# Pooled attention and a gated convolution on one core: the first k load as 32-bit words on SyncE's queue, v of batch 0 pooled on TensorE, and a new order of the queues

## Chip, cores and metric

The kernel runs on one core of one Trainium2 chip. The metric is the device time of one execution in microseconds (us), as the median of several runs. Five engines work side by side, each through its own list of instructions: PE (TensorE, matrix products), DVE (VectorE), ACT (ScalarE), POOL (GpSimd) and SP (SyncE). POOL and SP do almost nothing here but issue transfers (DMAs), which run on 16 DMA engines that all queues share.

## The reference

For each of 8 batches and 8 heads (576 rows, 64 columns), k and v are averaged over groups of 8 rows, so that there are 72 pooled rows. Attention of the 576 rows of q over these gives x; x goes through a gated convolution block.

```
k_p = k.reshape(B, H, Sp, pool, D).mean(axis=3)
v_p = v.reshape(B, H, Sp, pool, D).mean(axis=3)
scores = scale * np.matmul(q, k_p.transpose(0, 1, 3, 2))
attn = softmax(scores)
x = attn @ v_p, heads side by side: 8 x 576 x 512
h = np.maximum(x @ w_in, 0.0)                  # 512 -> 1024
conv_out = three taps along the rows, one weight per column and tap
out = (h * sigmoid(conv_out)) @ w_out          # 1024 -> 512
```

All inputs and the output are 32-bit floats; q, k and v have 9.4 MB each, 1.18 MB per batch.

## The kernel before, in words

**The work of one batch.** POOL issues loads of k, v and q that turn 32-bit floats into bf16 on the way (`load_k` L458, `load_v` L476, `load_q` L433). One row of the tile `k_b` or `v_b` holds a whole group of 8 rows (512 numbers), so pooling is three additions of halves on DVE: 512 to 256 (`pool8`, L632), to 128 (L639), to 64 (L649 for k, L695 for v). There are 576 such rows per batch, so a tile is 128 partitions by 5, with the last column of tiles half filled; rows 64 to 127 of it are zeroed by a memset (L612, L614). PE turns the sums of k (L662), and two copies put them into `kz` (L669), by 64 partitions each. q is regrouped in two halves of four heads (`qg`, L453), turned by PE (L735) and copied to `qT` (L744). Scores are PE products (L767, L769), their exponentials run on ACT (L775), and v enters through `vblk`, the pooled v times a mask (L700, L705). The products of attention and v are L792 and L796 ("av"); DVE divides them (L809, tile xx), PE turns them (L829) and a copy gives `xT` (L835). For late batches SP's transposing DMAs do the turning instead. Then come mm1 (`w_in`, L849 for batch 0 in parts, L872 for the others; relu on ACT), the convolution (on PE by diagonal matrices, L995, or on DVE and ACT, L918 to L945), the gate and its product on DVE into `gT` (L983), and mm2 (`w_out`, L1026) after each pair of batches, copied out of PSUM (L1049, L1039) and stored by SP (L1054, L1044). `gT` has two buffers, one for each second pair of batches; `gT[1]` is first written by batch 2.

**What sets the order.** Every operation is added to a planner (`pl.add`, L136) with a name, an engine, an assumed duration, the keys that it reads and writes, and, for a DMA, the packets. The planner (`order`, L176) picks in assumed time, on each engine, among the operations that can start within 0.02 us of the first one the one with the lowest rank. The ranks are a list of whole numbers, one for each operation in the order of its definition (L17 to L56). Operations that can run on ACT or on DVE (all copies out of PSUM, two of the three taps, the regrouping of q, the diagonal matrices) run on ACT if their names stand in the list "act" (L62), on DVE otherwise. The result is a fixed list of instructions for each engine. Where the assumed time has a gap on PE in the first 60 us, `warm` (L398) puts in products with a tile of zeros (L407), so PE shows no idle time there.

**The start, as it stands in the program.** POOL issues: q's rows 64 to 71, k's large part, k's tail, q's rows 0 to 63, half of v, the identity matrix (`ident`, L525, made by POOL), the tail of v in four, masks, the other half of v, q of batch 1, v's tail of batch 1, the first half of `w_in`, k and v of batch 1, the second half of `w_in`. SP issues the convolution weights (L528) and nothing else before the first store. At most 8 of POOL's loads are assumed to be under way at once (L223).

The lines that the change leans on for v are in the kernel before already, but no batch takes that way (`"vp"` is 0 for all eight):

```
for i in range(TP):
    nc.tensor.matmul(out=a, lhsT=ident, rhs=v_b[m][:, t0:t1, i * D:(i + 1) * D], start=i == 0, stop=i == TP - 1, skip_group_check=True)
...
copy_on(e)(out=vs[:, :, 0:D], in_=slot(key)[:, 0, 0:NT * D].rearrange("p (t d) -> p t d", d=D))
```

Eight products with the identity add up the eight slices of 64 columns in PSUM, in two parts (`vpm.0.0` for two tiles, `vpm.0.1` for three); the copy `vae.0` moves the sum to `vs`.

Of the kernel before, what the change touches and what calls it, by code (L numbers as in the profile page):

```python
# [9 lines left out]
FP32 = mybir.dt.float32  # L10
# [5 lines left out]
PARAMS = {  # L16
    "prio": (  # L17
        "6 14 12 18 16 17 25 33 43 49 53 56 58 61 63 40 38 59 46 54 60 9 32 28 34 31 24 22 "
        "37 29 20 42 39 27 21 35 41 5 2 3 47 11 8 0 30 4 7 13 44 15 36 19 23 10 1 69 "
        "90 75 80 84 62 182 143 45 52 55 57 64 65 51 48 73 78 70 74 26 66 67 77 50 79 72 89 86 "  # L20
        "85 111 88 83 94 82 87 68 71 76 81 93 91 102 126 124 92 115 97 103 112 101 118 99 96 105 98 114 "
        "100 133 119 107 131 109 116 125 113 136 121 110 146 104 141 148 151 157 132 164 120 108 117 106 129 127 123 128 "
        "95 165 174 179 186 189 167 218 172 178 169 173 185 188 175 181 194 201 203 224 234 202 210 211 219 204 184 208 "
        "207 217 221 213 226 233 241 245 231 236 239 244 249 122 130 142 134 150 158 156 161 160 168 152 137 155 138 154 "
        "176 192 135 140 145 149 139 144 147 162 163 170 153 159 171 180 216 200 265 267 220 230 190 196 205 212 193 197 "
        "232 240 247 255 261 266 183 191 177 187 209 225 199 206 195 229 198 237 253 250 277 260 286 293 316 324 328 338 "
        "349 335 355 348 359 370 215 166 223 228 248 257 262 291 304 317 235 214 242 256 238 243 227 222 246 274 287 303 "
        "312 309 321 345 310 327 344 362 334 351 326 340 365 377 381 393 402 380 385 386 411 413 379 387 389 406 412 398 "
        "399 401 408 415 395 400 404 410 417 252 254 289 299 306 320 264 251 270 278 294 322 318 353 292 263 271 305 330 "
        "297 276 302 308 313 339 341 268 273 275 288 300 307 284 283 290 296 311 315 323 258 269 282 285 331 301 280 298 "  # L30
        "329 347 342 350 336 361 371 382 388 384 392 403 407 428 450 461 476 494 507 272 259 295 314 325 319 337 358 369 "
        "374 352 357 360 368 367 376 363 366 281 333 346 343 364 354 418 423 448 457 391 396 427 419 463 451 459 477 480 "
        "484 491 449 489 483 502 528 485 493 495 525 512 501 503 508 522 530 519 524 532 539 542 442 460 488 498 482 506 "
        "475 505 509 520 533 556 576 583 439 444 437 473 447 446 456 478 455 465 469 474 479 486 504 515 429 435 534 541 "
        "443 440 420 454 453 550 552 514 521 529 537 548 569 546 555 570 579 586 591 578 603 616 638 629 685 696 640 656 "
        "674 708 717 279 332 356 375 373 378 383 422 434 426 397 390 414 425 466 470 467 481 464 416 513 452 538 431 421 "
        "430 433 436 511 517 523 531 540 543 497 500 551 549 559 526 564 604 608 590 596 599 610 624 601 607 620 639 647 "
        "611 623 625 642 646 626 631 637 645 641 547 499 568 575 572 585 600 581 584 614 627 630 636 635 573 580 577 561 "
        "588 594 622 598 609 617 652 644 671 675 605 618 562 571 633 612 628 597 643 650 666 651 665 664 593 606 587 595 "
        "634 654 649 632 658 663 673 677 684 676 699 716 721 724 751 746 761 782 756 767 776 784 802 394 409 438 432 424 "  # L40
        "441 445 471 405 487 554 510 592 544 613 496 589 468 615 545 458 462 472 535 565 707 710 718 679 722 729 709 715 "
        "686 694 738 687 736 768 744 692 749 760 743 704 763 798 754 706 759 777 757 732 788 789 667 683 648 659 690 668 "
        "725 680 705 728 731 735 747 809 661 669 681 688 682 697 698 719 720 733 753 765 774 780 657 662 693 703 727 711 "
        "670 714 726 745 739 758 783 795 734 740 712 702 750 742 755 741 769 775 808 810 814 822 845 860 861 872 874 886 "
        "911 903 912 916 518 582 553 574 492 516 527 557 560 567 558 678 566 700 621 372 619 490 563 713 536 653 655 660 "
        "672 785 790 771 779 766 772 773 762 786 801 793 811 804 815 803 812 819 818 806 817 816 825 841 843 846 851 839 "
        "848 850 856 796 807 813 821 824 829 827 823 834 837 835 844 936 855 832 840 826 830 842 828 849 858 847 862 883 "
        "871 885 890 857 863 820 831 865 833 864 836 873 889 888 884 893 898 853 869 838 852 868 854 867 859 876 881 896 "
        "899 905 891 918 926 941 929 948 950 961 972 966 980 969 977 982 602 689 695 770 764 781 748 730 723 752 737 701 "
        "691 778 792 787 878 879 900 917 791 797 800 805 794 799 925 945 931 935 927 930 934 940 937 947 978 959 946 943 "  # L50
        "953 955 956 968 962 967 880 892 895 902 908 913 897 915 919 924 939 928 949 954 906 920 914 951 922 952 944 965 "
        "960 964 971 974 994 983 870 875 882 887 901 904 907 894 923 910 921 932 938 942 866 877 958 963 909 970 957 933 "
        "973 975 984 979 986 989 1010 1019 1014 1021 1025 1023 1032 1038 1041 1055 1005 1012 1000 1004 1008 1009 1015 1007 1020 1018 1024 1022 "
        "1028 1033 981 991 976 985 1027 1034 988 990 993 995 999 1037 1039 1002 1016 992 1001 1030 1035 1003 1011 1006 1013 1017 1045 1042 "
        "996 998 987 997 1046 1044 1026 1029 1031 1036 1040 1047 1048 1043 1051 1052 1059 1050 1053 1049 1056 1054 1058 1060 1071 1057 1061 1062 "
        "1064 1063 1066 1069 1067 1068 1065 1070 "  # L56
# [5 lines left out]
    "act": (  # L62
        "dw1.0 dw1.1 dw4.0 dw5.0 dw6.0 dw6.1 kz.0.0 qg.0.0 qTe.0.0 qTe.0.3 xte.0.2 kz.1.0 "
        "kz.1.1 qg.1.0 qTe.1.0 xte.1.0 xte.1.2 xte.1.4 cp0.0.0 oe.0.0 oe.0.1 oe.0.2 oe.0.3 kz.2.0 "
        "qTe.2.0 qTe.2.1 qTe.2.2 xte.2.0 xte.2.1 xte.2.2 cp2.1.0 cp2.1.4 oe.0.4 oe.0.5 oe.0.6 oe.0.7 "
        "oe.0.8 kz.3.0 qTe.3.0 xte.3.0 xte.3.1 xte.3.2 cp0.2.0 cp0.2.1 cp0.2.3 cp2.2.5 oe.1.0 oe.1.1 "
        "oe.1.2 oe.1.3 kz.4.1 qTe.4.2 xte.4.0 xte.4.1 xte.4.3 cp0.3.0 cp2.3.0 cp2.3.2 cp0.3.4 cp0.3.5 "
        "cp2.3.6 oe.1.5 oe.1.6 oe.1.7 oe.1.8 kz.5.0 kz.5.1 cp2.4.1 cp2.4.3 cp0.4.7 oe.2.2 cp0.5.2 "
# [32 lines left out]
    "qs": [1, 0, 0, 0, 0, 0, 0, 0],  # L101
    "xw": 0,
    "qd": [0, 0, 0, 0, 0, 0, 0, 0],
    "vp": [0, 0, 0, 0, 0, 0, 0, 0],
}


# [7 lines left out]
class Planner:  # L115
# [60 lines left out]
    def order(self):  # L176
# [16 lines left out]
        ring = [0.0] * 4  # L193
# [964 lines left out]
```

## Time and profile before

| | us |
|---|---|
| median of 3 runs | 201.94 |
| lowest and highest of them | 201.72, 202.74 |
| the profiled execution, device time | 200.92 |
| its span, first to last instruction | 199.1 |
| PE busy in it | 190.8 |
| DVE busy in it | 171.0 |
| ACT busy in it | 167.0 |
| granted TensorE clock, share of full speed | 1.00 |

The profile comes from one execution. A row of its timeline gives the start and length of a stretch of like instructions, the engine, the line of the kernel, the operation, the tile written and the tile read, and in brackets how long the engine had been idle before and what released it. "L632" is line 632. The windows give, for each engine, the time that it was busy in a stretch with the number of its instructions, then the granted clock, the share of the 16 DMA engines' time in use (over 1 where packets overlap) and GB/s moved. The chain of work that ended last is followed back from the last instruction to whatever released each one. PE's busy time contains the products with zeros. Loads that convert count their bytes as bf16, half of what they read.

### The profile page before, as it was taken

Reading aid. Unit: us, or ns where it says so; the run is one execution under the profiler, and the core shown is the slowest. Engines: PE = TensorE matmul, PEld = TensorE weight load, DVE = VectorE, ACT = ScalarE, POOL = GpSimd, SP = SyncE. Lnnn points to the kernel's source line nnn. Section 1 sums busy time; section 2 is a strip of 40 time slices with the busy share of each in tenths; the row PEclk is TensorE's granted clock in tenths of the full one; section 3 lists DMA queues with packets and bytes.
Section 4 is the critical chain, followed back from the end, with each engine's and each line's share of the span. In section 5 each row is a group of like instructions: output and inputs, shape, how many; then the busy total and the mean of one; then the engine's idle time right before and its main releaser. Section 6 shows DMA issues by size and latency. Waiting matters only on the chain.

```text
span 199.1 us, 4491 instructions
## 1 busy us (share of the span) xinstructions
PE 190.8 (96%) x1737; PEld 128.9 (65%) x1737; DVE 171.0 (86%) x400; ACT 167.0 (84%) x282; POOL 47.5 (24%) x76
## 2 busy tenths in 40 slices
PE   5999999999999999999999999989999999999992
PEld 5888777777546576767756656547666565765541
DVE  3777999999999999999999999988889997755631
ACT  0677699999995499999999999995999999998410
POOL 7966431543233262761140000000000000000000
PEclk9999999999999999999999999999999999999999
DMA  3999999999999999999999966477112144502324
GB/s 39 185 185 200 204 204 193 207 206 200 195 204 250 268 217 207 159 217 121 113 116 117 70 211 161 85 189 188 28 35 83 65 129 87 211 3 77 135 106 158
DMA packets 52857, 30.00 MB, mean 151 GB/s; under 512 B 33484, under 2 KB 48356, under 8 KB 52836
## 3 DMA queue, kind: packets, MB, share of 16 engines
q0 software_dynamic: 32912, 16.73, 68.1%
q1 hardware_dynamic: 19924, 12.99, 26.9%
q8 instruction: 13, 0.21, 0.4%
q14 instruction: 8, 0.07, 0.1%
HBM read 33.44 MB, written 9.44 MB: 215 GB/s over the span
## 4 chain that ended last, share of the span: by engine, by line
PE 88%; DVE 7%; POOL 2%; DMA 1%; issue 1%; ACT 0%; POOLq 0%
PE psfB L1026 31%; PE psfA L872 25%; PE psfA L792 4%; PE psfA L767 4%; PE psfA L995 4%; PE pswA L407 3%; PE psbB L735 2%; PE psfB L849 2%; DVE xx L809 2%; PE psfA L849 2%; PE psfA L796 2%; PE psbB L829 1%; PE pswB L407 1%; PE psbA L829 1%; DMA xT<-xx 1%; PE psfA L769 1%
## 5 line engine op out<-in xcount | busy, mean ns | idle before, releaser
L1026 PE MATMUL psfB<-w_out,gT 128*128 128x512 bf16 (+1 forms) x282 | 65.5, 378 | 0.0
L872 PE MATMUL psfA<-xT,w_in 128*128 128x288 bf16 x448 | 59.2, 286 | 0.9 <-DMA xT<-xx 0.7
L872 PEld LDWEIGHTS <-w_in 128*128 128x128 bf16 x448 | 42.8, 98 | 14.8 <-issue 1.2
L1026 PEld LDWEIGHTS <-gT 128*128 128x128 bf16 x290 | 27.2, 98 | 29.0 <-issue 0.2
L878 ACT ACTIVATE hT<-psfA 128x576 bf16<-128x576 f32 x56 | 35.2, 651 | 2.2 <-PE psfA L872 2.0
L918 ACT ACTIVATE cv<-hT,cr 128x576 bf16<-128x576 bf16 x37 | 28.3, 779 | 0.2
L809 DVE TENSOR_TENSOR xx<-psfA,rr 128x512 bf16<-128x512 f32 (+1 forms) x40 | 26.8, 683 | 0.9 <-DMA xT<-xx 0.7
L920 DVE TENSOR_SCALAR cv<-hT,cr 128x576 bf16<-128x576 bf16 x71 | 23.9, 363 | 3.9 <-ACT tg L945 2.3
L775 ACT ACTIVATE attnT<-psfA 128x576 bf16<-128x576 f32 x40 | 25.1, 674 | 0.3 <-PE psfA L767 0.2
L983 DVE TENSOR_TENSOR gT<-tg,hT 128x1152 bf16<-128x1152 bf16 x32 | 23.7, 750 | 1.2 <-ACT tg L1002 0.8
L927 DVE TENSOR_TENSOR cv<-cv,hT 128x1152 bf16<-128x1152 bf16 (+1 forms) x31 | 20.8, 672 | 4.0 <-ACT cv L918 3.9
L945 ACT ACTIVATE tg<-cv,cn 128x576 bf16<-128x576 bf16 x31 | 23.2, 775 | 0.9 <-DVE cv L937 0.6
L937 DVE TENSOR_TENSOR cv<-cv 128x1152 bf16<-128x1152 bf16 (+1 forms) x31 | 20.8, 673 | 0.2
L1049 ACT COPY osb<-psfB 128x512 f32<-128x512 f32 x24 | 14.3, 595 | 7.4 <-PE psfB L1026 7.3
L945 ACT ACTIVATE tg<-cv,cs 128x576 bf16<-128x576 bf16 x23 | 17.5, 797 | 0.0
L792 PE MATMUL psfA<-vblk,attnT 128*128 128x130 bf16 (+1 forms) x160 | 15.7, 222 | 0.2
L407 PEld LDWEIGHTS <-zero 128*128 128x128 bf16 x206 | 13.0, 105 | 3.4 <-DVE zero L520 2.5
L792 PEld LDWEIGHTS <-attnT 128*128 128x128 bf16 (+1 forms) x160 | 11.0, 100 | 4.1 <-issue 1.8
L407 PE MATMUL pswA<-zero 128*128 128x128 bf16 x148 | 10.5, 236 | 2.5 <-DVE zero L520 2.5
L767 PE MATMUL psfA<-qT,kz 128*128 128x512 bf16 x64 | 12.3, 286 | 0.4 <-ACT attnT L775 0.4
L439 POOL DMA_DIRECT2D q<-in_q_dram x10 | 8.6, 863 | 12.1 <-DMA k_b<-in_k_dram 4.0
L796 PE MATMUL psfA<-vblk,attnT 128*128 128x130 bf16 (+1 forms) x80 | 11.2, 221 | 0.0
(94 smaller groups left out, 247.8 us busy)
## 6 DMA issues: line engine op xcount, KB each, us to landing
out_dram<-osb SPq DMA_DIRECT2D x14, 512.0 KB, 3.0
k_b<-in_k_dram POOLq DMA_DIRECT2D x8, 512.0 KB, 14.8
v_b<-in_v_dram POOLq DMA_DIRECT2D x7, 512.0 KB, 16.7
q_b<-in_q_dram POOLq DMA_DIRECT2D x4, 576.0 KB, 17.6
out_dram<-osb SPq DMA_DIRECT2D x7, 256.0 KB, 2.1
w_in<-in_moe_w_in_dram POOLq DMA_DIRECT2D x2, 512.0 KB, 11.4
w_out<-in_moe_w_out_dram POOLq DMA_DIRECT2D x2, 512.0 KB, 15.0
q<-in_q_dram POOLq DMA_DIRECT2D x8, 128.0 KB, 12.6
```

The lines of the kernel that those rows point to most:

```text
L407: nc.tensor.matmul(out=t, lhsT=zero[:, 0:P], rhs=zero[:, 0:P], start=True, stop=True)
L775: nc.scalar.activation(out=attnT[m][:, t, :], in_=slot(key).rearrange("p i x -> p (i x)")[:, 0:S], func=ACT.Exp, scale=1.0 / 64.0)
L792: nc.tensor.matmul(out=a[0:n, g, c * w:(c + 2) * w], lhsT=attnT[m][:, s, u0:u0 + n], rhs=vblk[m][:, 2 * s:2 * s + 2, :].rearrange("p x d - ...
L809: nc.vector.tensor_tensor(out=xx[i3][0:n].rearrange("p (g h e) -> p g h e", g=2, h=4), in0=av_view()[:, :, :, 0:D], in1=rr[i3][0:n].rearra ...
L872: nc.tensor.matmul(out=t[:, i, 0:HC], lhsT=w_in[:, c, f * P:(f + 1) * P], rhs=xT[m][:, c, i * HC:(i + 1) * HC], start=(c == 0), stop=(c == ...
L878: nc.scalar.activation(out=h_(b)[:, f, hs(b), 2:S + 2].rearrange("p (i x) -> p i x", i=2), in_=slot(key)[:, :, 0:HC], func=ACT.Relu)
L918: nc.scalar.activation(out=cv[y][:, kk // 2, z0:z1, :], in_=src, func=ACT.Copy, scale=sc)
L920: nc.vector.tensor_scalar(out=cv[y][:, kk // 2, z0:z1, :], in0=src, scalar1=sc, scalar2=None, op0=OP.mult)
L927: nc.vector.tensor_tensor(out=cv[y][:, 0, 0:n, :], in0=cv[y][:, 0, 0:n, :], in1=h_at(2), op=OP.add)
L945: nc.scalar.activation(out=tg[i3][:, zs[z0]:zs[z0] + z1 - z0, :], in_=cv[y][:, 0, z0:z1, :], func=ACT.Tanh if half else ACT.Sigmoid, scale ...
L983: nc.vector.tensor_tensor(out=o_, in0=tg[i3], in1=h2, op=OP.mult)
L1026: nc.tensor.matmul(out=a[:, 0, j0:j1], lhsT=g[:, c, t * P:(t + 1) * P], rhs=w_out[:, c, j0:j1], start=(c == 0), stop=(c == n_fb - 1), skip ...
```

## The change

Five things are edited.

1. k of batch 0 is loaded by SP as 32-bit words into `ks`, a view of the first 10 KB of each partition of `gT[1]`, in two DMAs (`ldk0.0` for 512 rows, `ldk0.t` for 64). A new memset `zks` clears the rows of `ks` that the tail leaves empty; the tail's DMA is ordered behind it.
2. The first addition of k of batch 0 reads these words and writes bf16 as before; the second and third are unchanged.
3. v of batch 0 takes the way over PE: 16 products and one copy in place of five additions on DVE.
4. The list of ranks and the list "act" are new as a whole. 49 names come into "act" that were not in it (one of them is the new `vae.0`) and 41 leave it. Sorted by rank, POOL's list now begins: q's rows 0 to 63, q's rows 64 to 71, half of v, one of v's tails, the identity matrix, the other three tails, the other half of v, masks, q of batch 1, the first half of `w_in`, k and v of batch 1 with its tail, the second half of `w_in`. SP's begins: the convolution weights, then the two k loads. Among the names that come into "act" are `kz.0.1`, `vae.0`, `oe.3.8.1` (the last copy of the output).
5. The planner's assumed time lets a DMA that SP issues in the first 4 us hold up the loads of POOL.

```diff
-    "vp": [0, 0, 0, 0, 0, 0, 0, 0],
+    "vp": [1, 0, 0, 0, 0, 0, 0, 0],
+    "kh": 1,
...
+                        if s < 4.0:
+                            ring[z] = max(ring[z], hring - 0.8)
...
+    ks = gT[1].rearrange("p f s -> p (f s)")[:, 0:NT * 1024].bitcast(FP32).rearrange("p (t e) -> p t e", t=NT)
...
+        if b == 0 and PARAMS["kh"]:
+            def fn(e):
+                nc.sync.dma_start(out=ks[:, 0:4], in_=src[0:512].rearrange("(t p) e -> p t e", p=P))
+            pl.add("ldk0.0", "SP", 0.43, fn, writes=[("ks", 0)], prio=prio, dma=(32, 0.085))
+
+            def fn(e):
+                nc.sync.dma_start(out=ks[0:64, 4], in_=src[512:576])
+            pl.add("ldk0.t", "SP", 0.43, fn, reads=["kzs"], writes=[("ks", 1)], prio=prio + 0.01, dma=(4, 0.085))
+            return
...
+            def fn(e):
+                nc.vector.memset(ks[64:P, 4], 0.0)
+            pl.add("zks", "DVE", 0.4, fn, writes=["kzs"], prio=-75)
...
-                pl.add(f"{name}p1.{b}.{x}", "DVE", 0.075 + 0.1334 * n, fn, reads=rk, writes=[("p1", y) for y in ys], prio=pr)
+                pl.add(f"{name}p1.{b}.{x}", "DVE", 0.075 + (0.267 if st_ else 0.1334) * n, fn, reads=rk, writes=[("p1", y) for y in ys], prio=pr)
...
+        if b == 0 and PARAMS["kh"]:
+            pool8(b, "k", [ks], pr, ((0, 5, (0, 1), [("ks", 0), ("ks", 1), "kzs"]),))
+        else:
+            pool8(b, "k", k_b, pr, ((0, 5, (0, 1), [("k", m, 0), ("k", m, 1)]),))
```

## The prediction, on record before the change was run

> **What bounds the kernel now.** I read the busy table and the chain of work that ended last, then windows, then the timeline of the first 25 us.
>
> ```profile
> PE 190.8 (96%) x1737; PEld 128.9 (65%) x1737; DVE 171.0 (86%) x400; ACT 167.0 (84%) x282; POOL 47.5 (24%) x76
> PE 88%; DVE 7%; POOL 2%; DMA 1%; issue 1%; ACT 0%; POOLq 0%
> ```
>
> PE carries 88% of the chain. But part of its busy time is filler: the group of L407 has 206 matmuls on the tile zero, and the timeline has all of them before 31 us. So there is a start in which PE waits and fills, then a dense stretch: in windows of 10 us PE is busy 10.00 from 40 on, save 9.83 at 90:100, 9.97 at 110:120, 8.65 at 130:140 and the last stores. A step in the first 30 us counts as far as it lets real matmuls start sooner. Next the windows of the start (last two columns: DMA share, GB/s):
>
> ```profile
> 2.00:3.00 1.00, 0.52 (x6) 0.52 (x7) 0.94 (x5) 0.00 (x0) 1.00 (x3) 1.00 0.16 17
> 3.00:4.00 1.00, 1.00 (x12) 1.00 (x11) 0.02 (x1) 0.00 (x0) 1.00 (x2) 1.00 0.55 74
> 4.00:5.00 1.00, 1.00 (x12) 1.00 (x10) 0.00 (x0) 0.00 (x0) 1.00 (x3) 1.00 0.82 95
> 6.00:7.00 1.00, 0.96 (x15) 0.93 (x16) 0.65 (x4) 0.42 (x1) 1.00 (x4) 1.00 1.27 208
> ```
>
> Transfers run at about 200 GB/s from 5 us on, but from 2 to 5 only 17, 74 and 95: 600 - 186 = 414 KB, 2.1 us at 200 GB/s, goes unused. Then the timeline:
>
> ```profile
> 0.81 0.43 SPq L528 DMA_DIRECT2D cw_raw<-in_moe_conv_w_dram  x1
> 1.43 0.74 POOL L445 DMA_DIRECT2D q_b<-in_q_dram  x1 [0.91 <-POOLq L1142]
> 2.16 0.78 POOL L468 DMA_DIRECT2D k_b<-in_k_dram  x1
> 3.46 0.73 POOL L445 DMA_DIRECT2D q_b<-in_q_dram  x1
> 8.45 0.82 DVE L632 TENSOR_TENSOR p<-k_b 128x1280 bf16<-128x1280 bf16 x1 [0.28 <-DMA k_b<-in_k_dram]
> 11.41 0.69 DVE L453 COPY q<-q_b 72x2048 bf16<-72x2048 bf16 x1 [0.33 <-DMA q_b<-in_q_dram]
> 13.75 0.65 ACT L775 ACTIVATE attnT<-psfA 128x576 bf16<-128x576 f32 x1
> 14.82 2.30 ACT L775 ACTIVATE attnT<-psfA 128x576 bf16<-128x576 f32 x4
> 17.09 0.40 PE L792 MATMUL psfA<-vblk,attnT 128*128 128x130 bf16 x4
> 21.70 0.82 PE L849 MATMUL psfA<-xT,w_in 128*128 128x384 bf16 x4
> ```
>
> k lands at 8.45 and the rest of q at 11.39; from there run regrouping, transposes, scores, five exponentials (the last ends at 17.12), av and, at 21.68, the first w_in product. Two chains meet there: the first half of w_in is issued at 12.76 and takes 8.9 us to land, 21.66. The second half, 15.60 + 13.8 = 29.4, lands before the other half of batch 0's mm1 at 30.86. So both the q chain and the DMA supply set the start.
>
> **k and q.** POOL loses two issues, 0.78 + 0.54; q's large part is issued at 1.43 in place of 3.46. On SP the k load stands behind cw_raw's 0.43, so at 1.24. A store alone (issued 182.25) puts its first packets at 183.0, and window 183:184 shows 332 GB/s; the packet records behind it show 95 packets of 2 KB per 0.5 us. So k's 576 packets begin at 2.0 and would alone take 3.0 us. Packets of a POOL load begin some 1.2 us after the issue ends (k now: 2.94, flow from about 4.1), so q's at 3.3. By then 240 of k's are through. How two queues share the engines is shown at 60:62, a store beside loads: 284 and 296 GB/s, half of the packets each, 100 per us. So the other 336 of k go by 6.7, landing about 7.2; q has 340 of 576 by then, the rest at 200 per us ends at 7.9, and with the lag of 0.95 that q has now (last packet 10.45, landing 11.39) it lands at **8.8, 2.6 sooner**. If k went first alone, k would land near 5.5 and q at the same 8.8: the sum of packets is equal.
>
> The Trainium skill speaks against this step: the page "DMA: Bandwidth & Descriptors", section "Issuing engines are not separate DMA queues", says that transfers issued from several engines run on the same 16 DMA engines, so that only issue time is saved. The mixed windows at 60:62 agree that packets interleave; the windows at 2:5 differ in that the engines stood partly idle.
>
> **The first add of k reads 32-bit words.** No 32-bit add of two SBUF operands is in the trace. Lower end: 0.82, as now. Upper end: L809's 0.685 for 512 elements with one 32-bit PSUM operand, scaled, 1.71. The bf16 adds of 512, 768 and 1280 (0.415, 0.558, 0.824) give 0.145 fixed; L809 less that is 1.05 ns an element, so 1.49, which I take: +0.67. The new memset of 64x512 words: 0.272 for 64x256, so 0.53, early on DVE; only the small k tail on SP waits for it, with nothing behind it on SP before the first store at 56.3.
>
> So k's sums go from 7.2 to 7.2 + 1.88 (now 8.45 to 10.33) + 0.67 = 9.75; q's half regrouping on DVE (0.69) stands behind, 10.45; scores follow 1.2 later as now (12.10 to 13.31), 11.65. On ACT the other half takes 8.8 + 1.9 = 10.7, then one kz copy (0.39), two qT copies (0.63 each) to 12.35, and five exponentials (0.575 apart) to 15.3.
>
> **v on PE.** Removed from DVE: 0.41 + 0.29 + 0.56 + 0.36 + 0.33 = 1.95. Added on PE: 8 matmuls of 128 columns and 8 of 192. Nearest rows: 0.058 a filler step of 128, and L849's 0.33 per 4 of 192, so 8 x 0.058 + 8 x 0.083 = 1.13; upper end 16 x 0.1 = 1.6. Fillers lie there (21 from 15.9, 24 from 10.85), so the cost is nothing while they cover it, up to 1.6 if it stands ahead of av. The copy out of PSUM is ACT's: between relu's 0.36 for 192 and 0.50 for 384, 0.45. It falls among the exponentials, so the last ends at **15.7 in place of 17.12: 1.4 sooner**. v itself, 576 packets behind q, is there by 12.
>
> **Supply.** The order q, v, q1, first w_in half, k1, v1, second half keeps the packets the same but for 128 (v1's tail) that go behind the first half. Of the 2.1 us unused I count 1.7, since the queue fills late: the second half at 27.7, the first (with 128 packets less, 0.6) at 19.3. mm1 is then set by the q chain, 21.68 - 1.4 = 20.3, and its second half by supply, 1.7 sooner. I take **1.5** for the start of the dense stretch.
>
> **Engine split and order.** With the duration of each kind of copy in the rows, the new assignment gives ACT 5.8 us more (72.6 for 66.8) and DVE 4.7 less; by batch ACT gets +1.1, +0.1, +1.0, +1.0, +2.7 for 0 to 4, then -0.7, -3.1, +0.8. PE's real work is as before, and it sets the dense stretch. ACT has 5.14 idle at 60:70, where its copies wait for PE. I cost the split and the new order at nothing, within -1.5 (the PE gaps at 90:100 and 130:140 closed, 0.17 + 1.35) and +3.1 (below). The last two halves of the output, now on ACT and DVE one behind the other (195.46, 195.87), both go to ACT: 0.37 for 0.42, nothing.
>
> **Sum.** The profiled execution took 200.92, 199.1 of it span: 200.92 - 1.5 = 199.4. The median of the runs is 201.94, 1.02 above that execution; the same 1.5 off it gives **200.4**. For this kernel about 0.5%, 1.0 us, can be told from no change.
>
> **Rivals.**
> - *The new order fits better all along*: 1.5 and the two PE gaps, 1.52, together 3.0: 198.9. For it: DVE, on the chain from 92.24 to 98.36, is relieved by 4.7 + 1.95 - 0.67 - 0.53 = 5.5. Against: after 140 PE has no gap to close. Chance 0.12.
> - *The k load gains issue time alone, or waits*: a store issued at 56.33 put its first packets only at 60.0, behind the loads queued. If k at the start waited 3.7 as well, it would begin at 4.9, land at about 9, and with 2.55 of sums, kT and kz (1.0) give scores at 12.7 for 13.31: 0.6 sooner. If only POOL's 1.32 is saved, q lands at 10.07, and the two ACT copies put into the path (0.39 + 0.45) leave 0.5. 201.4. Against: at 2 us no load is queued yet. Chance 0.20. By that section of the Trainium skill the time would be this rival's.
> - *ACT becomes the bound*: at 70:130 it is idle 0.20 + 0.09 + 0.11 + 0.11 + 0.03 + 0.05 = 0.6. Batches 3 and 4 put 3.7 more on it. If the added copies stand ahead of relus and exponentials that PE waits for, PE is late by 3.7 - 0.6 = 3.1, and 201.94 - 1.5 + 3.1 = 203.5. It decides once more than 0.6 of the 3.7 falls there and PE shows gaps on ACT. Against: the idle 5.14 at 60:70 can take some, and PE can be given other work. Chance 0.23.
> - *Forecast*: 0.45; its own range is 199.6 to 201.3, from 0.6 to 2.3 gained (k's add at either end, v's matmuls covered or not).
>
> Faster by over 0.5%: the forecast but for its upper edge and the first rival, 0.55; within: the second and that edge, 0.22; slower: the third, 0.23. The range must reach into both sides: 198.7 to 203.5.
>
> **What would show it.** First add of k starting at 5.5 to 7.5 and lasting near 1.5; regrouping of q at about 8.8; av at about 15.7; first w_in product at about 20.3; the second half of mm1 some 1.7 sooner than 30.86; fewer L407 matmuls. Wrong, if k lands after 8, if ACT waits for the k copy ahead of q's regrouping, or if PE shows new gaps released by ACT after 60 us, with the 1.5 given back there.

## The result, and the profile after

Twelve runs of the changed kernel on one chip have a median of 203.50 us, twelve runs of the kernel before beside them 202.25: the ratio is 1.0062, 95% interval 1.0033 to 1.0091. The change made the kernel **slower by 0.6%**, some 1.3 us; 1.5 less had been forecast. The profiled execution took 203.15, its span 201.3 (before: 200.92 and 199.1).

The busy table and the shares of the chain that ended last:

```profile
PE 189.9 (94%) x1687; PEld 127.5 (63%) x1687; DVE 167.3 (83%) x388; ACT 173.2 (86%) x290; POOL 45.7 (23%) x74
PE 52%; ACT 17%; DMA 15%; DVE 9%; issue 3%; POOL 2%; ACTq 0%; DVEq 0%; POOLq 0%
```

ACT has 6.2 more and DVE 3.7 less, about as the prediction counted (5.8 and 4.7). But PE, 88% of the chain before, is 52% now, and DMA went from 1% to 15%: 8% of it is a load of `w_in`, 5% a load of q. The windows of the start, of after:

```profile
2.00:3.00 1.00, 0.00 (x0) 0.00 (x0) 0.78 (x5) 0.00 (x0) 1.00 (x3) 1.00 0.33 66
3.00:4.00 1.00, 0.98 (x10) 0.98 (x11) 0.56 (x3) 0.00 (x0) 1.00 (x3) 1.00 0.49 152
4.00:5.00 1.00, 1.00 (x10) 0.80 (x7) 0.41 (x3) 0.00 (x0) 0.93 (x3) 1.00 1.00 389
6.00:7.00 1.00, 1.00 (x12) 1.00 (x11) 1.00 (x7) 0.99 (x2) 1.00 (x6) 1.00 1.16 254
10.00:15.00 5.00, 4.29 (x82) 3.90 (x79) 2.92 (x7) 3.12 (x4) 3.71 (x5) 1.00 1.07 125
30.00:35.00 5.00, 3.97 (x47) 2.81 (x46) 4.06 (x12) 4.35 (x11) 0.85 (x1) 1.00 1.35 189
```

and the last two stretches of before:

```profile
10.00:15.00 5.00, 5.00 (x93) 4.35 (x91) 3.75 (x13) 4.00 (x6) 3.48 (x8) 1.00 1.21 184
30.00:35.00 5.00, 5.00 (x60) 3.80 (x58) 4.97 (x14) 4.97 (x11) 0.95 (x2) 1.00 1.29 193
```

The unused transfer time from 2 to 5 us is filled, as meant (66, 152 and 389 GB/s for 17, 74 and 95; k's are 32-bit bytes, so counted double). Five us later it is lost again: 125 GB/s for 184 at 10:15. At 30:35 PE, full before, is idle for 1.03. The timeline of after:

```profile
1.31 1.43 POOL L448 DMA_DIRECT2D q_b<-in_q_dram  x2 [0.80 <-POOLq L1165]
1.31 0.42 SPq L468 DMA_DIRECT2D gT<-in_k_dram  x1
1.79 0.56 SPq L472 DMA_DIRECT2D gT<-in_k_dram  x1
8.72 1.49 DVE L651 TENSOR_TENSOR p<-gT 128x1280 bf16<-128x1280 f32 x1 [0.50 <-DMA gT<-in_k_dram]
11.29 1.09 POOL L448 DMA_DIRECT2D q_b<-in_q_dram  x1 [3.54 <-DMA q_b<-in_q_dram]
11.32 0.69 DVE L456 COPY q<-q_b 72x2048 bf16<-72x2048 bf16 x1 [1.11 <-DMA q_b<-in_q_dram]
11.93 0.48 DVE L659 TENSOR_TENSOR p<-p 128x640 bf16<-128x640 bf16 x1
12.45 0.49 DVE L672 TENSOR_TENSOR ksum<-p 128x640 bf16<-128x640 bf16 x1
15.86 0.65 ACT L798 ACTIVATE attnT<-psfA 128x576 bf16<-128x576 f32 x1
15.91 0.81 POOL L522 DMA_DIRECT2D w_in<-in_moe_w_in_dram  x1
18.74 0.40 PE L815 MATMUL psfA<-vblk,attnT 128*128 128x130 bf16 x4
23.65 0.81 PE L872 MATMUL psfB<-xT,w_in 128*128 128x384 bf16 x4
```

Read it as two chains, and beside them this row of before:

```profile
8.29 0.75 POOL L488 DMA_DIRECT2D v_b<-in_v_dram  x1 [0.27 <-DMA k_b<-in_k_dram]
```

**q and k:** q is issued at 1.31, 2.15 sooner than before, and regrouped at 11.32, where it was 11.41. k's two loads land at 7.2 and 8.6, and its first addition starts at 8.72 for 8.45. DVE's list has q's regrouping between the first and second addition of k: it waits 1.11 for q, and the sums end at 12.94 (10.33 before), the first exponential starts at 15.86 (13.75). **Supply:** POOL stands 3.54 until q has landed; eight loads have been issued by then (two of q, six of v), and in e1 below, too, the ninth waits for q. Before, k's landing let POOL go on after 0.27. q of batch 1 is issued at 11.29 (9.28), and the second half of `w_in`, issued at 15.91, takes 15.9 and lands at 31.8 (29.4). The first mm1 product comes 1.95 later than before. The last copy of the output starts at 198.08 for 195.87. Counted back from the last product, and without those on the tile zero and those of v, PE is 1.2 us behind before at 30 us, 1.7 at 40, 1.9 from 60 to 90 and 2.3 from 160 on. So about half of what this profile loses is lost by 30 us and some 0.6 after 40.

### The profile page after: what moved, and what is told of

The parts are those of the page before. It is cut to its first block, busy times and chain, and to the rows that moved or that the text cites. A ratio compares the mean times of both kernels' runs of the same rounds, so it can differ in the third digit from the quotient of the medians.

```text
span 201.3 us, 4396 instructions
## 1 busy us (share of the span) xinstructions
PE 189.9 (94%) x1687; PEld 127.5 (63%) x1687; DVE 167.3 (83%) x388; ACT 173.2 (86%) x290; POOL 45.7 (23%) x74
## 4 chain that ended last, share of the span: by engine, by line
PE 52%; ACT 17%; DMA 15%; DVE 9%; issue 3%; POOL 2%; ACTq 0%; DVEq 0%; POOLq 0%
PE psfB L1049 21%; PE psfA L895 15%; DMA w_in<-in_moe_w_in_dram 8%; ACT hT L901 5%; DMA q_b<-in_q_dram 5%; ACT tg L968 3%; PE psfA L815 3%; ACT cv L941 3%; PE psfA L1018 3%; DVE xx L832 3%; DMA xT<-xx 2%; PE psfA L790 2%; DVE cv L950 2%; PE psfB L872 2%; PE psfA L819 1%
## 5 line engine op out<-in xcount | busy, mean ns | idle before, releaser
L1049 PEld LDWEIGHTS <-gT 128*128 128x128 bf16 x290 | 27.2, 98 | 28.8 <-DVE gT L1006 0.3
L943 DVE TENSOR_SCALAR cv<-hT,cr 128x576 bf16<-128x576 bf16 x74 | 26.7, 380 | 5.1 <-ACT hT L901 3.2
L968 ACT ACTIVATE tg<-cv,cn 128x576 bf16<-128x576 bf16 x34 | 25.9, 779 | 1.5 <-DVE cv L960 1.1
L941 ACT ACTIVATE cv<-hT,cr 128x576 bf16<-128x576 bf16 x34 | 25.7, 775 | 0.8 <-DVE cv L960 0.6
L1072 ACT COPY osb<-psfB 128x512 f32<-128x512 f32 x26 | 15.2, 586 | 4.7 <-PE psfB L1049 4.7
L968 ACT ACTIVATE tg<-cv,cs 128x576 bf16<-128x576 bf16 x20 | 15.3, 783 | 0.0
L410 PEld LDWEIGHTS <-zero 128*128 128x128 bf16 x140 | 10.6, 117 | 3.7 <-DVE zero L534 3.0
L410 PE MATMUL pswA<-zero 128*128 128x128 bf16 x107 | 9.3, 264 | 3.0 <-DVE zero L534 3.0
```

The source lines that it names most:

```text
L941: nc.scalar.activation(out=cv[y][:, kk // 2, z0:z1, :], in_=src, func=ACT.Copy, scale=sc)
L943: nc.vector.tensor_scalar(out=cv[y][:, kk // 2, z0:z1, :], in0=src, scalar1=sc, scalar2=None, op0=OP.mult)
L968: nc.scalar.activation(out=tg[i3][:, zs[z0]:zs[z0] + z1 - z0, :], in_=cv[y][:, 0, z0:z1, :], func=ACT.Tanh if half else ACT.Sigmoid, scale ...
L1049: nc.tensor.matmul(out=a[:, 0, j0:j1], lhsT=g[:, c, t * P:(t + 1) * P], rhs=w_out[:, c, j0:j1], start=(c == 0), stop=(c == n_fb - 1), skip ...
```

## The experiments

Eighteen kernels ran, in five sets; each ratio is to runs of the kernel before on the same chip. "q" is DVE's regrouping of q, "exp" the first exponential, "w_in" the landing of its second half (issue plus time to landing), "end" the start of the last output copy; these four come from one profiled execution each.

| run | ratio, interval | q | exp | w_in | end |
|---|---|---|---|---|---|
| before | 1 | 11.41 | 13.75 | 29.4 | 195.87 |
| after | 1.0062, 1.0033 to 1.0091 | 11.32 | 15.86 | 31.8 | 198.08 |
| b1_k_on_sp | 0.9969, 0.9939 to 0.9999 | 11.36 | 14.27 | 28.8 | 196.58 |
| d3_half_of_k | 0.9954, 0.9920 to 0.9988 | 11.16 | 14.26 | 30.4 | 197.32 |
| a4_k_on_pool | 1.0045, 1.0012 to 1.0078 | 11.65 | 16.19 | 31.1 | 197.68 |
| a5_v_on_dve | 1.0058, 1.0022 to 1.0094 | 11.04 | 15.80 | 31.8 | 198.66 |
| c3_no_k_load | 0.9908, 0.9877 to 0.9939 | 9.55 | 13.80 | 28.4 | 196.40 |
| a6_four_loads | 1.0053, 1.0014 to 1.0093 | 12.76 | 17.87 | 29.0 | 198.45 |
| a1_sums_first | 1.0192, 1.0146 to 1.0237 | 11.35 | 22.03 | 31.9 | 202.30 |
| a2_one_tail | 1.0019, 0.9979 to 1.0058 | 11.20 | 17.71 | 29.4 | 199.21 |
| a3_both | 1.0203, 1.0162 to 1.0245 | 11.35 | 21.50 | 29.4 | 201.66 |
| c1_sums_first | 1.0060, 1.0026 to 1.0095 | 11.26 | 17.04 | 31.8 | 198.35 |
| d2_sums_kz | 1.0073, 1.0037 to 1.0108 | 11.42 | 15.37 | 30.5 | 198.34 |
| d1_sums_kz_tail | 1.0027, 0.9988 to 1.0066 | 11.55 | 19.29 | 29.6 | 199.09 |
| e1_no_v_tails | 0.9942, 0.9897 to 0.9987 | 11.03 | 17.02 | 28.4 | 196.64 |
| e4_sums_kz_no_v_tails | 0.9948, 0.9908 to 0.9988 | 11.41 | 15.24 | 28.9 | 196.56 |
| e2_sums_kz_no_v5 | 1.0049, 1.0018 to 1.0079 | 11.42 | 16.29 | 32.2 | 198.73 |
| e3_no_v5 | 0.9996, 0.9969 to 1.0022 | 11.31 | 17.80 | 31.6 | 198.40 |
| f1_v_tails_on_sp | 1.0074, 1.0038 to 1.0110 | 12.00 | 17.59 | 29.4 | 198.20 |
| f2_half_of_k_v_tails_on_sp | 1.0025, 0.9993 to 1.0057 | 11.66 | 14.57 | 28.3 | 196.50 |

One profile is a coarse tool here. After and e3 issue the same program until past 50 us, yet their first exponentials stand at 15.86 and 17.80: at 10:20 the granted clock was 1.00 in the one and 0.79, then 0.53, in the other. So verdicts rest on ratios, and landmarks say where to look.

The ratios hold something of the clock too. Of the executions of after and of the variants built on it, 87 of 167 had a mean granted clock below 0.995 (0.979 to 0.992); of those of before, b1, d3 and f2 it was 1 of 183. In the 13 kernels that had both kinds, the ones below took 1.0 us longer on average (79 against 58 executions, those that count for the ratios). In after itself they did not, 203.58 (7) for 203.50 (5), so the clock does not make its loss. But it enters comparisons between variants: below 0.995 were 10 of 12 in a2, d1 and f1, 5 of 10 in e1, 2 of 10 in e4, none in c3. What lowers it was not tested.

### The parts of the change, each by itself

b1_k_on_sp: the kernel before, with k of batch 0 by SP as 32-bit words and nothing else.

```diff
-                nc.gpsimd.dma_start(out=k_b[m][:, 0:4, d], in_=src[0:512, c]...)
+                (nc.gpsimd if b else nc.sync).dma_start(out=(k_b[m] if b else ks())[:, 0:4, d], in_=src[0:512, c]...)
...
```

> The kernel before with the one part alone: k of batch 0 as 32-bit words by SP into the idle buffer, first addition on these words, the new memset; every other instruction stands in the old order. Theory A (k's load keeps the engines to itself until about 6, so that q, although issued at 2.2 in place of 3.5, lands no sooner than now): q lands at 10.5 to 11.3, k's first addition starts at about 8.7 and its sums end at about 11.1, just ahead of q's regrouping; time within 0.5 of the kernel before, 202.2. Rival (q was late only through the new order of loads): q lands near 9, scores 1.5 or more sooner, time 201 or less.

The way of k is not what costs: 0.9969, some 0.6 us gained at the middle of an interval that just misses 1. q, though issued sooner, was regrouped at 11.36; its queue's first packets of 1 KB came at 5.6, behind k's.

a4_k_on_pool: the changed kernel with k by POOL again, converted on the way, ahead of q.

```diff
-                nc.sync.dma_start(out=ks[:, 0:4], in_=src[0:512].rearrange("(t p) e -> p t e", p=P))
+                nc.gpsimd.dma_start(out=k_b[0][:, 0:4, :], in_=src[0:512].rearrange("(t p) e -> p t e", p=P))
...
```

> The changed kernel with k of batch 0 loaded by POOL as bf16 ahead of q, as in the kernel before; no new memset; every other instruction in the new order. Theory A: k lands near 8.4, q at 11.4 or a little later, k's second addition still stands behind q's regrouping, so the first exponential stays at 15.5 to 16 and the time at the changed kernel's, ratio 1.004 to 1.008: the new order is what costs, not the way of k. Rival (the load on SP itself costs, by holding up q and the loads behind it): ratio 1.000 or less.

1.0045: without the new way of k the loss is there. What a4 shares with the change are its ranks, its split of ACT and DVE, and v on PE.

a5_v_on_dve: the changed kernel with v of batch 0 added on DVE.

```diff
-                        nc.tensor.matmul(out=a, lhsT=ident, rhs=v_b[m][:, t0:t1, i * D:(i + 1) * D], ...)
...
-                copy_on(e)(out=vs[:, :, 0:D], in_=slot(key)[:, 0, 0:NT * D]...)
+                five additions of v on DVE, as before
```

> The changed kernel with v of batch 0 pooled by DVE's five additions again, at the place where the copy out of PSUM stood; no v products on PE. Theory A: v's products ahead of q's turning cost PE 0.4 to 1.0 at 11.5 to 15, but the supply sets the dense stretch, so the time stays at the changed kernel's, ratio 1.004 to 1.008. If v's products are what makes the start late: 1.002 or less.

1.0058 against 1.0062: v on PE costs nothing that shows. By elimination the loss sits in the **new order**, ranks and split together: no run has one without the other, and none has the new order with both k and v as before.

### What k's load does to q

c3_no_k_load: the changed kernel without k's large load of batch 0.

```diff
-                nc.sync.dma_start(out=ks[:, 0:4], in_=src[0:512].rearrange("(t p) e -> p t e", p=P))
...
```

> The changed kernel without the large part of k's load on SP; its tail is loaded, and the first addition reads the last of the five tiles five times over (so k's sums are not k's). It shows when q lands with no load of SP ahead of it. If k's load keeps q's packets off the engines, q's packets begin at about 3.0 in place of 5.9 and q lands at about 8.0 to 8.5 in place of 11.3; the rest follows 2 to 3 sooner, time about 200.5. If the load of q is slow by itself (POOL's way to the engines), it lands at 10.5 or later, time 202.5 to 203.5.

```profile
1.30 1.43 POOL L448 DMA_DIRECT2D q_b<-in_q_dram  x2 [0.79 <-POOLq L1165]
8.05 0.87 POOL L448 DMA_DIRECT2D q_b<-in_q_dram  x1 [0.29 <-DMA q_b<-in_q_dram]
8.50 1.88 ACT L456 COPY q<-q_b 72x2048 bf16<-72x2048 bf16 x1
```

That is c3's timeline: the same issue at 1.30, but q has landed by 8.05, 3.2 sooner than in after, where POOL goes on at 11.29. The packet records behind both traces show why. In c3 q's packets of 1 KB start at 3.0. In after the first comes at 5.9. Until then k's packets of 2 KB go alone, 31 and 9 per half us (by their ends) from 2.5 to 3.5, then 45, then 97 to 100 from 4.0 to 6.0, and only then are the two queues mixed. k's one DMA of 512 rows, 32 packets for each of the 16 engines, went through whole. Time: 0.9908, 3.1 us less than the change. That is not the price of q's wait alone: 1 MB less is moved, and leaving out 640 KB later on was worth 0.5 and 1.3 us (e2, e3 below).

a6_four_loads: the changed kernel with that load cut in four.

```diff
-                nc.sync.dma_start(out=ks[:, 0:4], in_=src[0:512].rearrange("(t p) e -> p t e", p=P))
+                for t in range(4): nc.sync.dma_start(out=ks[:, t], in_=src[P * t:P * t + P])
```

> The changed kernel with k's large load on SP cut into four DMAs of 128 rows. If an engine serves a whole DMA of one queue before it turns to the other, q's packets now come in between from about 3.5, k lands later (9 or more) and q sooner (10 or less). If SP's queue goes first whatever the size, packets of q still begin near 6 and q lands at 11.3; time as the changed kernel, within 0.5.

```profile
1.30 1.79 SPq L468 DMA_DIRECT2D gT<-in_k_dram  x4
10.88 1.90 ACT L456 COPY q<-q_b 72x2048 bf16<-72x2048 bf16 x1 [2.29 <-DMA q_b<-in_q_dram]
11.35 1.49 DVE L651 TENSOR_TENSOR p<-gT 128x1280 bf16<-128x1280 f32 x1 [3.12 <-DMA gT<-in_k_dram]
```

With 8 packets for each engine in a DMA, q's packets come in from 3.9, after two of the four (256 packets). Then q's queue goes alone, 248 packets between 4.5 and 5.9, and only from there do the last two alternate with it half and half; k lands 2.6 later than in after. q gains 0.4 on ACT, DVE stands 3.12 for k: 1.0053, nothing gained. So the sharing half and half that the prediction took from 60:62 exists, but not from the start on, and not beside one large DMA that came first.

d3_half_of_k: the kernel before, with two of k's five tiles by SP.

```diff
+                b or nc.sync.dma_start(out=ks()[:, 0:2], in_=src[0:256].rearrange("(t p) e -> p t e", p=P)); t0 = 0 if b else 2
-                nc.gpsimd.dma_start(out=k_b[m][:, 0:4, d], in_=src[0:512, c]...)
+                nc.gpsimd.dma_start(out=k_b[m][:, t0:4, d], in_=src[t0 * P:512, c]...)
...
```

> The kernel before with two of k's five tiles, 256 rows, loaded by SP as 32-bit words, the other rows by POOL as before; the first addition of k in two parts (512 words, 768 bf16); all else in the old order. If SP's load holds up POOL's only while it runs, 256 rows are through by 4.2 (as the first two of the four loads were in a6), when POOL's packets hardly flow yet; the rows behind them land 0.6 to 1.2 sooner, q at 10.2 to 10.8 in place of 11.4, and the time falls by 0.5 to 1.0, ratio 0.995 to 0.998. If it costs POOL's loads as much as it takes off them, 1.000.

0.9954: **the lowest ratio of a version that computes all of the reference**, ahead of both kernels, though its interval overlaps that of b1. In the packet records all but 8 of its 256 SP packets are through by 4.0, where POOL's loads begin, so it fills the unused time and holds up little. Its profiled execution shows none of the gain (exp 14.26, end 197.32) and q only 0.25 sooner, less than expected, so how the gain comes about is not shown; the verdict is that of the runs.

### DVE's list: k's sums ahead of q

a1_sums_first: the changed kernel with the second and third addition of k right behind the first, kT behind them, the two kz copies behind q's regrouping.

```diff
+moves = [("kp2.0.0 ksum.0", "behind", "kp1.0.0"), ("kT.0", "behind", "ksum.0"), ("kz.0.0", "behind", "qg.0.4"), ("kz.0.1", "behind", "kz.0.0")]
```

> The changed kernel with one thing moved: on DVE the second and third addition of k stand right behind the first, ahead of q's regrouping; on PE the turning of k's sums stands ahead of v's products; the two kz copies follow q's regrouping. Theory A (the start is late by two chains: k's sums stuck behind q's regrouping on DVE, and a supply of loads that is late by itself): the first scores move from 15.40 to about 13.9 and av from 18.68 to about 17.2, but the second half of w_in still lands near 31.8, so the time falls by no more than 0.5, to about 203.0. Theory B (the queue on DVE alone makes the start late): 1.5 sooner, 202.0. Theory C (the new split of copies, ACT later on, costs the time): the start is sooner, the end is not, 203.5.

1.0192, by a fault of the edit: kT went ahead of the products with zeros that cover PE's wait, and the waits of the first 30 us show PE standing for it.

```profile
PEld L685 <- DVE ksum L672: 6.5, 1, 6.5
PE psbB L685 <- DVE ksum L672: 6.4, 1, 6.4
```

The 83 zero products ran behind kT instead, and the scores came at 22. c1_sums_first is the same with them ahead of kT.

```diff
+pl.gaps[kT.0] = pl.gaps.pop(vpm.0.0)
```

> The edit of a1 again, with the 83 fillers that stand on PE ahead of v's first products now standing ahead of the turning of k's sums, so that PE is not filled after it. Theory A (two late chains): first exponential at about 14.9 in place of 15.86, since qT's last group still waits for q's regrouping on ACT; the second half of w_in still near 31.8; time 202.7 to 203.2, ratio to the kernel before 1.002 to 1.005. Theory B (the queue on DVE alone): ratio 0.998 or less. Theory C (the later split of copies): ratio 1.006 as the changed kernel.

1.0060. k's sums now end at 11.32, 1.6 sooner, and nothing follows: q's turning waits 1.09 for a kz copy that stands on ACT behind the regrouping. d2_sums_kz, on top of c1, puts both kz copies of batch 0 on DVE.

```diff
-                copy_on(e)(out=kz[m][r]...
+                copy_on(e if b else "DVE")(out=kz[m][r]...
```

> As c1 (k's sums, and the turning of them with its fillers, ahead of q's regrouping), and both kz copies on DVE, so that neither waits for q's regrouping on ACT. Theory A (the supply of loads sets the dense stretch): first exponential at 14.5 to 15.2 in place of 15.86, first w_in product about 1 sooner, but the second half of w_in still lands at 31.8; time as the changed kernel, ratio 1.003 to 1.007. Theory B (the scores set it): ratio 1.000 or less.

Scores 0.5 sooner than in after, `w_in` 1.3 sooner, and the ratio 1.0073. So DVE's list alone is **not** the cause. The lead was given back at 78 us in this profile:

```profile
61.62 16.85 DMA v_b<-in_v_dram
78.57 0.83 DVE p L651
```

These two pieces of d2's chain that ended last are a load of v of batch 5 and DVE's addition that waits 1.61 for it. In after the same addition starts at 78.13 without that wait. A sooner start met a load that came no sooner.

e2_sums_kz_no_v5 and e3_no_v5 leave that load out, of d2 and of after.

```diff
+                    b == 5 or nc.gpsimd.dma_start(out=v_b[m][:, c0:c1, d], in_=src[0:P, c0:c1, e0], **op)
...
```

> The version with k's sums first and the kz copies on DVE, without the load of v of batch 5 (its v is that of batch 3, left in the buffer). In the version itself DVE waits 1.61 for that load at 78.57, the chain of waits goes back through its 16.9 us of transfer, and the lead of 1.3 to 1.7 over the changed kernel is gone behind it. Theory: with the load gone, the add starts at about 77.0, PE shows no gap of 0.9 at 80:90, the lead over the changed kernel at exp 25 stays at 1.0 or more, and the time is 0.8 to 1.7 less than the changed kernel. Rival (another limit stands close behind, such as the k load of batch 4 or POOL's eight loads under way): the wait moves to the next load, and the time is within 0.4 of the changed kernel.

> The changed kernel itself without the load of v of batch 5, as the counterpart. There the add of that v starts at 78.13 without a wait for its load, so the theory expects at most 0.5 less than the changed kernel (less traffic for the loads behind it). Rival (transfers pace the dense stretch everywhere, and 640 KB less of them are worth 2 to 3 us wherever they go): 1.0 or more less.

The theory failed: 1.0049 for 1.0073 in d2, 0.9996 for 1.0062 in after. The load is worth 0.5 us where DVE waited for it and 1.3 where it did not, with intervals that overlap. The rivals fit better: 640 KB less to move helps wherever it is, and the wait at 78 was one limit among several. d2's lead in its one profile may be partly chance as well: e2, the same program up to there, had its first exponential 0.9 later.

### POOL's stand and the supply of w_in

a2_one_tail: the four small loads of v's last rows as one, so that POOL has three loads fewer under way.

```diff
-                        nc.gpsimd.dma_start(out=v_b[m][32 * c + 16:32 * c + 32, 4, d], in_=src[P:P + 16, c, e0], **op)
+                        if c == 2: nc.gpsimd.dma_start(out=v_b[m][:, 4, d], in_=src[P - 16:P + 16, :, e0].rearrange("y c e -> c y e"), **op)
```

> The changed kernel with the tail of v of batch 0 loaded by one DMA in place of four, so that POOL has three loads fewer outstanding when it comes to q of batch 1. Theory A: POOL no longer sits from 7.8 to 11.3 until q has landed; q of batch 1 is issued near 6.5, the DMA engines do not run dry at 13 to 14, the second half of w_in lands at about 29.7 in place of 31.8, the PE gaps of 1.5 at 25:35 shrink; scores stay at 15.4. Time 0.3 to 0.8 less, about 203.0. Theory B: no change, since scores are as late. Theory C: no change, 203.5.

1.0019: between the two kernels, and its interval tells it from neither. POOL issues sooner (`w_in` lands at 29.4), but the one load comes in late: the second v product waits for it until 15.30, and mm1 starts 2.7 later than in after, at a granted clock of 0.86 and 0.50 in 10:20 for 1.00. a3_both has this with a1's edit, d1_sums_kz_tail with d2's.

> Both edits together: k's chain ahead of q's regrouping, and one DMA for v's tail. Theory A: both late chains are mended, scores near 13.9 and w_in's second half near 29.7; the time falls by about 1.8, to 201.7, more than the sum of the two alone. Theory B: as the first edit alone, 202.0. Theory C: 203 or more, the lag coming back after 60 us.

> As d2, and v's tail in one DMA, so that POOL issues q of batch 1 near 6.5 and does not wait until q lands. Theory A: the second half of w_in lands at 28 to 29 and scores are at 15 or less; both chains are mended, ratio 0.994 to 0.999, about 1.5 less than d2. Theory B: as d2. Theory C (the later split of copies costs): the start is sooner by 1.5 or more but the ratio stays above 1.003.

a3, 1.0203, carries a1's fault. d1, 1.0027, has the v product at 16.89 after a wait of 2.53 and the last output copy at 199.09 in its profile. These three can't tell supply from a late v or from the clock (0.66 in d1 at 15:20).

e1_no_v_tails leaves the four small loads out of after, e4_sums_kz_no_v_tails out of d2.

```diff
-                        nc.gpsimd.dma_start(out=v_b[m][32 * c + 16:32 * c + 32, 4, d], in_=src[P:P + 16, c, e0], **op)
+                        pass
```

> The changed kernel without the four small loads of v's last 64 rows of batch 0 (that part of v is left out of the result). Theory A (the start of the dense stretch is set by the supply of w_in, and POOL stood from 7.75 to 11.29 because its first loads had not landed): q of batch 1 is issued before 6.5 in place of 11.29, the transfers do not run dry at 13 to 14, the second half of w_in lands before 30.5 (31.83 in the changed kernel), and relu 15 starts over 1.0 sooner than 38.72, although scores still start at about 15.4. Time 1.0 to 1.5 less than the changed kernel if it lasts to the end, 0 to 0.7 less if the later v load takes it back. Theory B (DVE's order of k's sums and q's regrouping alone): nothing moves, relu 15 at 38.5 to 39, time that of the changed kernel within 0.3.

> The same without the four small v loads, on the version whose k sums come ahead of q's regrouping and whose kz copies are on DVE. Theory A with both chains: scores at about 14.9, w_in's second half before 30.3, relu 15 at 36.5 to 37.2 (37.44 in that version, 38.72 in the changed kernel), and most of it given back where v of batch 5 is waited for, near 78: end within 0.7 of the changed kernel. If nothing takes it back: 1.5 to 2.2 less than the changed kernel.

POOL's timeline of e1:

```profile
5.53 0.86 POOL L448 DMA_DIRECT2D q_b<-in_q_dram  x1
6.38 0.77 POOL L522 DMA_DIRECT2D w_in<-in_moe_w_in_dram  x1
11.02 1.00 POOL L502 DMA_DIRECT2D v_b<-in_v_dram  x1 [2.57 <-DMA q_b<-in_q_dram]
12.73 0.77 POOL L522 DMA_DIRECT2D w_in<-in_moe_w_in_dram  x1
```

q of batch 1 goes out 5.8 sooner, the first half of `w_in` 6.0, the second 3.2, landing at 28.4; the stretch 10:15 moves 202 GB/s. The ratio is 0.9942: the whole loss and as much again is gone, 2.4 us, though the first exponential comes at 17.02, later than in after; e1's profile ran at a clock of 0.86 and 0.80 in 10:20, so that landmark says little. e4 has the same time, 0.9948. So the four loads mattered, by their places or by themselves, and DVE's list did not show. ("relu 15" is the last relu of batch 0; its start came only 0.64 sooner in e1's profile, for over 1.0 expected.)

f1_v_tails_on_sp keeps the bytes and takes only the places: the four loads go to SP as 32-bit words, and one copy on POOL makes bf16 of them. f2_half_of_k_v_tails_on_sp does it to d3.

```diff
-                        nc.gpsimd.dma_start(out=v_b[m][32 * c + 16:32 * c + 32, 4, d], in_=src[P:P + 16, c, e0], **op)
+                        nc.sync.dma_start(out=vt()[32 * c + 16:32 * c + 32], in_=src[P:P + 16, c])
...
+                    t0 and nc.gpsimd.tensor_copy(out=v_b[m][:, 4], in_=vt())
```

> The changed kernel with the four small v loads on SP, as 32-bit words into the idle buffer behind k's, and one copy on POOL that makes bf16 of them; nothing is left out. Theory (the four places that these loads hold among POOL's eight under way cost the change its time, and not the 64 KB): POOL issues q of batch 1 before 6.5 and the first half of w_in before 7.5, w_in's second half at about 13.5 landing near 29, and the time is that of the run without them, 0.994 of the kernel before, up to 0.998 if the second v product waits for the copy behind POOL's v load of batch 1 (copy at 12 to 13). Rival (the bytes or the late landing cost it): 1.003 to 1.009, as the change itself.

> The kernel before with two of k's five tiles on SP as 32-bit words (0.9954 in its run) and its four small v loads on SP in the same way, with a copy on POOL. The theory expects POOL's first half of w_in 2 to 3 us sooner than 12.47, mm1's first 0.5 to 1.0 sooner than 22.23, and a time of 0.988 to 0.994. Rival (in that order k's landings free POOL's places early enough, q of batch 1 is issued at 9.23 there): 0.994 to 0.998, no more than half of k alone gives. Slower than 0.998 if DVE's second add of v waits for the copy with the exponentials' inputs behind it.

Neither gained: 1.0074, as the change itself, and 1.0025, above d3's 0.9954. f1's timeline:

```profile
11.99 1.00 POOL L502 DMA_DIRECT2D v_b<-in_v_dram  x1 [3.43 <-DMA q_b<-in_q_dram]
12.00 0.69 DVE L456 COPY q<-q_b 72x2048 bf16<-72x2048 bf16 x1 [1.43 <-DMA q_b<-in_q_dram]
12.99 0.62 POOL L706 CAST v_b<-gT 128x512 bf16<-128x512 f32 x1
13.12 0.85 DVE L672 TENSOR_TENSOR ksum<-p 128x640 bf16<-128x640 bf16 x1
14.27 0.78 POOL L522 DMA_DIRECT2D w_in<-in_moe_w_in_dram  x1
```

The places came free as expected (`w_in` lands at 29.4, 2.4 sooner than in after). But v's rows, now in SP's queue behind k's, mixed with q's packets until 9.5, and q lands 0.7 to 1.0 later than in after and e1; beside the copy on POOL DVE's sum of k took 0.85 for 0.49; k's sums end at 13.98. So the places alone don't explain e1's gain: the same transfers put elsewhere at the start cost as much.

**What is settled and what is open.** Settled: the loss is not in the way of k (b1), not in v on PE (a5), not in DVE's list alone (c1, d2, e4 beside e1), and present without the new way of k (a4). Supply goes with it, though not strictly. Of the six versions with `w_in` down by 29.0, four (b1, c3, e1, e4) are faster than before; f2 and a6, in which v's rows or k mix with q from SP's queue, are not. The four at 29.4 to 29.6, where before has it too (a2, a3, d1, f1), are not either, each with an edit that does harm elsewhere. Of the six with it at 30.5 or later and nothing left out (after, a1, a4, a5, c1, d2), none is; d3, at 30.4, is. Open: which part of the new order costs the time, since ranks and split were not tried apart; how much of e1's 2.4 us is POOL's places and how much the four transfers themselves, which were not measured apart in a version that leaves q alone; and which of the later limits (v of batch 5, the transposing DMAs into xT, on which PE waits 1.3 at 130:140 in after and 2.2 at 120:158 in e4) takes back a sooner start.

## Why the prediction was wrong, point by point

**The step that failed** is "lands at 8.8, 2.6 sooner" in the part on k and q. It split the engines half and half between SP's and POOL's packets from 3.3 us on, by the mixed windows at 60:62. Measured: q's queue has its first packet at 5.9, 2.6 later, and q lands at 11.3, 2.5 later. c3 and a6 show it as k's one large DMA going first. A second error is in the same sum: k's packets were counted at 95 per half us from 2.0 on; by 4.0, 85 had come in place of 380, 1.6 us behind. k was forecast whole at 7.2; its large part is down at 7.2 and its tail at 8.6. That the large part fits is luck: its late stream and the engines that it did not share make up for each other. The prediction's own sign of being wrong, k after 8, came true.

- *The first add* was right: 1.49 forecast, 1.49 measured, also the 1.24 for SP's issue (1.31).
- *"k's sums go from 7.2"*: they start at 8.72, because the add waits for k's tail too. Its 64 packets are in the forecast's 576, but they came in mixed with q's, behind the large part.
- *"q's half regrouping on DVE stands behind, 10.45"* was the wrong way round. The rank list puts it between k's first and second addition, which costs 1.72 (kp2 at 11.93 where 10.21 was free). Mending it (c1, d2) did not move the time, so the step was wrong but not decisive.
- *v on PE at nothing* held (a5).
- *Supply, 1.7 sooner*: the second half of `w_in` came 2.4 later. The sum of packets was right; that POOL can have only so many loads under way, and that k's landing had let it go on at 8.29 before, was not in it. With k gone from POOL's queue, it goes on when q lands, at 11.29. This term is off by 4.1 and has the wrong sign; without the four small loads, with q of batch 1 and `w_in` out some 6 sooner, 2.4 were gained (e1).
- *Split and order at nothing*: with v on PE, a4 has 1.0045, 0.9 us, on the side of loss; the term's bounds (-1.5 to +3.1) held it.

**The rivals.** The time, 203.5, is that of "ACT becomes the bound", but hardly by its mechanism: it asked for 3.1 of PE's time behind 60 us. From 40 to 190 PE is busy 147.81 for 148.45 before, and ACT ends one of its waits in each kernel, after's first here:

```profile
PE psfA L815 <- ACT hT L901: 0.6, 1, 0.6
PE psfA L767 <- ACT attnT L775: 0.4, 1, 0.4
```

Some 1.7 of the 2.3 stand by 40 us. ACT's share of the chain, 17%, may mean that it is close behind PE. Nearest was the second rival, "gains issue time alone, or waits", though it was q that waited and not k, and it was priced as a small gain, 201.4, for q at 10.07. By the page "DMA: Bandwidth & Descriptors" of the Trainium skill, section "Issuing engines are not separate DMA queues", only issue time is saved; b1 agrees (0.9969, q no sooner at 11.36), and d3, at 0.9954, gains as little.

The same page, section "Queues, rings and completion order", says that an engine takes turns between its queues a whole packet of descriptors at a time, typically 9 to 17, at most 64. After's 32 rows per engine going through in one turn agree with the ceiling, not with the typical size; a6's first turns, 256 and then 248 packets over 16 engines, some 16 each, agree with both.

## What to carry to other kernels

When a load is moved to another queue, ask of each queue what then lands first: POOL, with eight loads under way, went on when its oldest landed, so taking away its quickest load stopped it for longer (3.54) than the issues save (1.32). A large DMA that comes first may hold the engines until it is through; a part that fits into the idle time (256 rows here) gained as much or more without that. And price a new order by its landings, queue by queue, before pricing its instructions.

## What the runs showed of the hardware that was not expected

- One DMA of 32 packets of 2 KB for each engine kept the other queue's packets out for its whole length (after: POOL's first at 5.9, b1: 5.6, c3: 3.0). Four DMAs of 8 let them in after two (a6: 3.9); POOL's then went alone, 248 packets, and from 6.5 us on the queues alternated, 46 to 49 packets of each per half us.
- Before k's stream ran at 97 per half us it stood nearly still: 9 packets in 3.0 to 3.5 in after; in d3, with half the rows, 101 ran in the same stretch.
- Beside a copy on POOL an addition on DVE took 0.85 for 0.49 (f1), and a tiny operation 0.75 where d3 has 0.16 (f2); another tiny one, beside POOL's DMA issues alone, took 0.59 for 0.16 (f2). The page "SBUF — State Buffer" of the Trainium skill, section "Terms", says that DVE and GpSimd share a pair of ports that one of them locks for a whole instruction; the two rows beside the copy agree.
- Two executions of the same program up to there (after, e3) had the first exponential 1.9 apart, at a granted clock of 1.00 and 0.53 in 15:20, and the last relu of batch 0 only 0.8 apart.
